# One row of wq loaded in three uneven pieces, and used last

## The chip, the cores and the metric

The kernel runs on one core of one Trainium2 chip. The metric is the device time of one execution in microseconds (us). Three runs of the kernel before took 138.65, 138.70 and 138.75 us; the median is 138.7 us. The profile is one execution taken by the hardware profiler; a time without a unit below is us from the start of its span.

The core has a matrix engine (TensorE, PE), three engines for elementwise work (VectorE or DVE, ScalarE or ACT, GpSimd or POOL) and SyncE (SP), which here only issues transfers. Transfers between the chip's memory and the on-chip buffer of 128 partitions run on 16 DMA engines. A transfer is issued on the queue of SP or ACT and is then split over DMA engines; when an engine has done its share, it adds one count to the transfer's semaphore.

## The reference

One decoding step of a transformer block, batch 4, one new token, model width 1024, 32 query heads in 4 groups of key/value heads, head width 128, all in bfloat16. Cut to what matters:

```python
q = layernorm(x) @ wq                     # wq: 1024 x 4096
k, v = k_cache[:, :, -2048:], v_cache[:, :, -2048:]
p = softmax(q . k / sqrt(128))            # 8 query heads to each kv head
h = x + (p . v) @ wo                      # wo: 4096 x 1024
n = layernorm(h)
out = h + (silu(n @ w1) * (n @ w3)) @ w2  # w1, w3: 1024 x 3584; w2: 3584 x 1024
```

Each weight and each used key and value is read once, 55.6 MB in all, and there are only four rows of activations to multiply them by.

## The kernel before, in words

All large operands go through one tile, `ring`, of five units of 16,384 bfloat16 numbers per partition. A unit is filled again when what it held has been used. In order, SP issues (through the helper `load`, whose only statement is line 124, so that all these transfers carry that line): row 0 of wq (1 MB), rows 1 to 7 of wq (7 MB), four loads of k (2 MB each), two of v, then two more of v, wo (8 MB), w1 and w3 (7 MB each), and w2 in six pieces of 13, 8, 4 and 2 rows and two half rows. "Row" here is an index inside a partition: wq's 1024 input features are dealt so that partition p holds features 8p to 8p+7, and row kc holds feature 8p+kc of every partition; a row of wq is 8,192 bytes in each of the 128 partitions.

The order is written by hand (`manual_schedule`): each engine runs its instructions in program order, and a wait holds all behind it on that engine. SP waits before a load until the unit's old content has been read, and until the semaphore that it will use is free again; there are eight semaphores for transfers, given out in turn to all transfers in the order of the program, x's and the stores' included.

The program's stages:

- x is loaded from ACT's queue into `x_nat` (line 135: four groups of four rows of 512 bytes), transposed (line 218) and normalized in `layernorm_T` (lines 189 to 214), whose result `xn_T` is done by line 211.
- The query (lines 229 to 240): for each of the eight rows kc, two halves of the heads and four column groups, one matmul of 512 columns, 64 in all, accumulating over kc in `q_ps`. In row 0 `start` is set, in row 7 `stop`.
- q is copied (line 243), transposed (line 246) and spread into `Qm` (line 253).
- For each batch element 64 blocks of keys are transposed on PE (line 267) and copied back into the ring (lines 269 and 271), then scores (line 290), softmax (line 331), spreading and transposing of the probabilities (lines 344 and 366) and the output (line 381).
- wo (line 468), the second layernorm, gate and up projections (line 494), and the product with w2 (lines 538 and 554), of which the last rows accumulate in `y_ps`. Then the result is added up (lines 577, 578 and 582) and stored by four small transfers (line 587).

Where the places in the ring meet the change: wq lies in units 0 and 1, rows 0 and 1 in the first half of unit 0. The third and fourth load of v (`load_values(1)`, line 241) overwrite unit 0, the third one rows 0 and 1, the fourth rows 2 and 3. The transfer of w1 begins in unit 1, that of w3 in unit 3, where wo was.

Of the kernel before, what the change touches and what calls it, by code (L numbers as in the profile page):

```python
# [10 lines left out]
P = 128  # L11
# [10 lines left out]
def kernel(  # L22
# [29 lines left out]
    KC = D // P  # L52
# [15 lines left out]
    wq_v = A_wq.rearrange("(p kc) n -> p kc n", kc=KC)  # L68
# [29 lines left out]
    def at(unit, *shape):  # L98
        o = unit * UNIT
        view = ring[:, o : o + int(np.prod(shape))]  # L100
        if len(shape) == 1:
            return view
        names = "abc"[: len(shape)]
        return view.rearrange(
            f"p ({' '.join(names)}) -> p {' '.join(names)}", **dict(zip(names, shape))
        )

    wq_s = at(0, KC, NQ)
# [14 lines left out]
    def load(dst, src):  # L123
        nc.sync.dma_start(out=dst, in_=src)  # L124
# [8 lines left out]
    x_nat = act.tile([P, DQ], BF16)  # L133
    nc.gpsimd.memset(x_nat[:], 0.0)
    nc.scalar.dma_start(out=x_nat[::S, :], in_=x_flat.rearrange("b (c n) -> c b n", c=C))
    for r in (slice(0, 1), slice(1, KC)):
        load(wq_s[:, r, :], wq_v[:, r, :])
    for b in range(B):
        load(k_s[:, b].rearrange("p j d -> p (j d)"), k_v[:, :, b])
    load_values(0)  # L140
# [85 lines left out]

    q_ps = ps.tile([P, 2, REP // 2, Dh], FP32, tag="scA")
    HALF = REP // 2
    for kc in range(KC):
        for hf in range(2):  # L230
            for c in range(C):
                o = (2 * c + hf) * HALF * Dh
                nc.tensor.matmul(  # L233
                    q_ps[R * c : R * c + R, hf],
                    lhsT=xn_T[:, kc, :],
                    rhs=wq_s[:, kc, o : o + HALF * Dh],
                    start=(kc == 0),
                    stop=(kc == KC - 1),
                    tile_position=(0, R * c),
                )  # L240
    load_values(1)
# [198 lines left out]
    for e in range(C):  # L440
# [4 lines left out]
            start=(e == 0),  # L445
            stop=(e == C - 1),
# [6 lines left out]
    for i in range(2):  # L453
        for k in range(2):
# [5 lines left out]
                start=(k == 0),  # L460
                stop=False,
# [3 lines left out]
    for t in range(T):  # L465
        row = wo_s[:, t].rearrange("p (k i n) -> p i k n", k=2, i=2)
        for i in range(2):
# [4 lines left out]
                start=False,  # L472
                stop=(t == T - 1),
# [60 lines left out]
    for w, n in zip(w2_s[:NE], W2B[:NE]):  # L534
        for ff in range(n):
            row = w[:, ff].rearrange("p (k i n) -> p i k n", k=2, i=2)
            for i in range(2):
# [4 lines left out]
                    start=(fc == 0),  # L542
                    stop=(fc == FE - 1),
# [3 lines left out]
    for k in range(2):  # L547
        part = h1[2 * R * k : 2 * R * k + 2 * R, :]
        nc.vector.tensor_tensor(out=part, in0=early_ps[:, k], in1=part, op=ALU.add)
    for m, (w, n) in enumerate(zip(w2_s[NE:], W2B[NE:])):  # L550
        for ff in range(n):
            for t, c, size in ((0, 0, DH), (0, 1, DH), (1, 0, DH), (1, 1, DH), (2, 2, DQ), (2, 3, DQ)):
# [5 lines left out]
                    start=(fc == FE),  # L558
                    stop=(fc == FC - 1),
# [4 lines left out]
        if m == 0:  # L564
# [4 lines left out]
                start=False,  # L569
                stop=False,  # L570
# [3 lines left out]
    for k in range(2):  # L574
        part = slice(2 * R * k, 2 * R * k + 2 * R)
# [44 lines left out]
```

## Time and profile before

| what | us |
|---|---|
| median of three runs | 138.7 |
| the profiled execution's own time | 138.7 |
| its span, first to last instruction | 136.7 |
| PE busy | 74.8 (55%) |
| DVE busy | 49.9 (37%) |
| ACT busy | 28.8 (21%) |
| POOL busy | 15.3 (11%) |
| SP's DMA queue, share of 16 engines' span | 95.3% |
| row 0 of wq, from issue to landing | 4.6 |
| rows 1 to 7 of wq, from issue to landing | 21.2 |
| granted TensorE clock, mean | 0.912 |

The profiled execution is 2.0 us longer than its span; that part lies around the first and the last instruction. A line of the chain reads: start, duration, and what the time went to, an engine's instructions with tile and line or a transfer. A line of the waits names who waited for whom, the total, how often, and the longest. SPq is SP's queue of transfers. Where a line says "q_ps L233 x64", 64 instructions of line 233 of the kernel write the tile `q_ps`.

Besides the views the text uses the trace's records of DMA packets (start, duration, queue and size of each) and the times at which transfers added counts to their semaphores. The records do not name the DMA engine, but a packet starts within some nanoseconds of the end of the one before it on the same engine.

### The profile page before, as it was taken

Reading aid. Unit: us, or ns where it says so; the run is one execution under the profiler, and the core shown is the slowest. Engines: PE = TensorE matmul, PEld = TensorE weight load, DVE = VectorE, ACT = ScalarE, POOL = GpSimd, SP = SyncE. Lnnn points to the kernel's source line nnn. Section 1 sums busy time; section 2 is a strip of 40 time slices with the busy share of each in tenths; the row PEclk is TensorE's granted clock in tenths of the full one; section 3 lists DMA queues with packets and bytes.
Section 4 is the critical chain, followed back from the end, with each engine's and each line's share of the span. In section 5 each row is a group of like instructions: output and inputs, shape, how many; then the busy total and the mean of one; then the engine's idle time right before and its main releaser. Section 6 shows DMA issues by size and latency. Waiting matters only on the chain.

```text
span 136.7 us, 1762 instructions
## 1 busy us (share of the span) xinstructions
PE 74.8 (55%) x762; PEld 40.6 (30%) x762; DVE 49.9 (37%) x50; ACT 28.8 (21%) x32; POOL 15.3 (11%) x41
## 2 busy tenths in 40 slices
PE   0000044959999986029966875994184000946471
PEld 0000011439957852014423323341042000413240
DVE  0000110006526363989799920004100594090022
ACT  3000130025968495104000000000405400000000
POOL 7300060000000000000176333000200000000000
PEclk9999999999999999955999999599959955599999
DMA  4999697999999999998978979969799798999960
GB/s 163 497 454 538 269 537 307 432 417 451 408 432 436 412 436 408 436 585 360 556 326 364 556 326 475 520 285 537 336 470 508 302 520 372 384 423 432 384 245 2
DMA packets 2795, 55.70 MB, mean 408 GB/s; under 512 B 324, under 2 KB 612, under 8 KB 740
## 3 DMA queue, kind: packets, MB, share of 16 engines
q1 hardware_dynamic: 2752, 55.58, 95.3%
q8 instruction: 6, 0.10, 0.3%
q10 hardware_dynamic: 36, 0.01, 0.0%
q14 instruction: 1, 0.01, 0.0%
HBM read 55.58 MB, written 0.01 MB: 407 GB/s over the span
## 4 chain that ended last, share of the span: by engine, by line
DMA 59%; PE 28%; DVE 6%; ACT 3%; SPq 1%; issue 1%; DVEq 0%
DMA ring<-in_B_w_dram 43%; DMA ring<-in_A_wq_dram 15%; PE kt_ps L267 9%; PE sc_ps L290 5%; PE q_ps L233 4%; PE o_ps L381 4%; PE gate L494 3%; DVE P L344 2%; DVE PT L366 2%; ACT ring L271 1%; PE small L381 1%; DVE ring L269 1%; SPq L124 1%; DVE rmax L302 1%; ACT q_sb L243 1%
## 5 line engine op out<-in xcount | busy, mean ns | idle before, releaser
L271 ACT COPY ring<-kt_ps 128x2048 bf16<-128x2048 bf16 x8 | 14.6, 1866 | 7.1 <-PE kt_ps L267 7.1
L267 PE MATMUL kt_ps<-ident,ring 128*128 128x128 bf16 x256 | 15.0, 219 | 0.6 <-DVE Qm L253 0.5
L267 PEld LDWEIGHTS <-ring 128*128 128x128 bf16 x256 | 14.4, 98 | 2.6 <-issue 2.6
L269 DVE COPY ring<-kt_ps 128x2048 bf16<-128x2048 bf16 x8 | 9.8, 1225 | 9.3 <-PE kt_ps L267 9.3
L398 POOL TENSOR_TENSOR o<-od 128x256 f32<-128x256 f32 x4 | 6.8, 1695 | 54.2 <-DVE od L389 54.2
L193 PE MATMUL sums_ps<-both,mean_f 128*128 128x64 f32 x4 | 1.1, 366 | 18.9 <-ACT both L191 18.9
L494 PE MATMUL up<-ring,n_T 128*32 128x448 bf16 x64 | 4.7, 467 | 12.2 <-DMA ring<-in_B_w_dram 12.2
L494 PEld LDWEIGHTS <-n_T 128*32 128x32 bf16 x128 | 4.2, 121 | 20.2 <-DMA ring<-in_B_w_dram 12.7
L344 DVE TENSOR_TENSOR P<-p,gmask 128x2048 bf16<-128x2048 bf16 x4 | 9.1, 2278 | 0.8 <-ACT p L331 0.8
L381 PEld LDWEIGHTS <-PT 128*128 128x128 bf16 x64 | 6.7, 107 | 9.0 <-issue 1.9
L366 DVE STREAM_TRANSPOSE PT<-P 128x2048 bf16<-128x2048 bf16 x4 | 9.2, 2306 | 0.1
L515 DVE RECIPROCAL eg<-eg 128x896 f32<-128x896 f32 x1 | 5.8, 5753 | 9.5 <-ACT eg L514 9.5
L468 PE MATMUL y_ps<-ring,oP 128*32 128x512 bf16 x64 | 8.8, 442 | 0.1
L233 PE MATMUL q_ps<-ring,n_T 128*32 128x512 bf16 x64 | 6.6, 587 | 3.8 <-DMA ring<-in_A_wq_dram 2.0
L381 PE MATMUL o_ps<-ring,PT 128*128 128x512 bf16 x32 | 8.6, 430 | 0.0
L290 PE MATMUL sc_ps<-ring,Qm 128*32 128x512 bf16 x64 | 7.6, 604 | 0.4 <-DVE ring L269 0.4
L538 PE MATMUL early_ps<-ring,hg_T 128*32 128x512 bf16 x42 | 4.9, 379 | 5.1 <-DMA ring<-in_B_w_dram 5.1
L381 PE MATMUL small<-ring,PT 128*128 128x512 bf16 x32 | 7.2, 379 | 0.7 <-DVE rinv L362 0.7
L193 PEld LDWEIGHTS sums_ps<-both,mean_f 128*128 128x128 f32 x4 | 0.8, 248 | 19.4 <-issue 16.9
L494 PE MATMUL gate<-ring,n_T 128*32 128x448 bf16 x64 | 4.6, 458 | 3.2 <-DMA ring<-in_B_w_dram 3.2
L577 ACT CAST res<-y_ps 64x128 bf16<-64x128 f32 x1 | 0.3, 259 | 26.3 <-PE y_ps L554 26.3
L218 DVE STREAM_TRANSPOSE x_T<-x_nat 128x256 bf16<-128x256 bf16 x1 | 0.6, 626 | 13.0 <-DMA x_nat<-in_A_x_dram 13.0
(81 smaller groups left out, 62.5 us busy)
## 6 DMA issues: line engine op xcount, KB each, us to landing
ring<-in_B_w_dram SPq DMA_DIRECT2D x2, 7168.0 KB
ring<-in_A_k_cache_dram SPq DMA_DIRECT2D x4, 2048.0 KB, 25.6
ring<-in_A_v_cache_dram SPq DMA_DIRECT2D x4, 2048.0 KB, 42.9
ring<-in_A_wq_dram SPq DMA_DIRECT2D x1, 7168.0 KB, 21.2
ring<-in_B_w_dram SPq DMA_DIRECT2D x1, 3328.0 KB
ring<-in_B_w_dram SPq DMA_DIRECT2D x1, 2048.0 KB
ring<-in_A_wq_dram SPq DMA_DIRECT2D x1, 1024.0 KB, 4.6
ring<-in_B_w_dram SPq DMA_DIRECT2D x1, 1024.0 KB, 28.1
```

The source lines that it names most:

```text
L233: nc.tensor.matmul(q_ps[R * c : R * c + R, hf], lhsT=xn_T[:, kc, :], rhs=wq_s[:, kc, o : o + HALF * Dh], start=(kc == 0), stop=(kc == KC - 1),
L267: nc.tensor.transpose(out=kt_ps[:, jj], in_=blocks[:, jj, :], identity=ident[:])
L269: nc.vector.tensor_copy(out=blocks, in_=kt_ps[:])
L271: nc.scalar.copy(out=blocks, in_=kt_ps[:])
L290: nc.tensor.matmul(sc_ps[b // 2][R * q : R * q + R, b % 2], lhsT=Qm[:, b, g * R : (g + 1) * R], rhs=kT[:, b, g, q], start=(g == 0), stop=( ...
L344: nc.vector.tensor_tensor(out=P4[:], in0=stage.pop(("p1", b))[:].rearrange("p (x o) -> p x o", o=1).to_broadcast([P, JR * L5, Hkv]), in1=g ...
L366: nc.vector.transpose(out=PT[:].rearrange("p j h -> p (j h)"), in_=stage.pop(("P4", b))[:].rearrange("p x g -> p (x g)"),)
L381: nc.tensor.matmul(o_ps, lhsT=PT[:, i * JM : (i + 1) * JM, :].rearrange("p j h -> p (j h)"), rhs=v_s[b][:, i * JM : (i + 1) * JM, :], star ...
L398: nc.gpsimd.tensor_tensor(out=o2[:], in0=od[:, :2], in1=od[:, 2:], op=ALU.add)
L468: nc.tensor.matmul(y_ps[R * i : R * i + R], lhsT=oP[:, t, :], rhs=row[:, i], start=False, stop=(t == T - 1), tile_position=(0, R * i), ski ...
L494: nc.tensor.matmul(out_ps[hf][R * c : R * c + R, :], lhsT=hn_T[:, kc, :], rhs=cols[:, kc, c, hf], start=(kc == 0), stop=(kc == KC - 1), ti ...
L515: nc.vector.reciprocal(out=eg[:], in_=eg[:])
```

## The change

Row 0 of wq is no longer loaded as one transfer of 128 partitions. Partitions 0 to 95 are loaded first, then rows 1 to 7 in one transfer as before, and then partitions 96 to 120 and 121 to 127 of row 0, each as a transfer of its own, ahead of the keys. The query's matmuls run over rows 1, 2, ... 7 and then 0; `start` and `stop` are set by the position in that order.

```diff
-    for r in (slice(0, 1), slice(1, KC)):
-        load(wq_s[:, r, :], wq_v[:, r, :])
+    PARTS = (slice(0, 96), slice(96, 121), slice(121, P))
+    load(wq_s[PARTS[0], :1, :], wq_v[PARTS[0], :1, :])
+    load(wq_s[:, 1:, :], wq_v[:, 1:, :])
+    for part in PARTS[1:]:
+        load(wq_s[part, :1, :], wq_v[part, :1, :])
     for b in range(B):
         load(k_s[:, b].rearrange("p j d -> p (j d)"), k_v[:, :, b])
     load_values(0)
...
-    for kc in range(KC):
+    for m in range(KC):
+        kc = (m + 1) % KC
         for hf in range(2):
             for c in range(C):
                 o = (2 * c + hf) * HALF * Dh
...
                     rhs=wq_s[:, kc, o : o + HALF * Dh],
-                    start=(kc == 0),
-                    stop=(kc == KC - 1),
+                    start=(m == 0),
+                    stop=(m == KC - 1),
                     tile_position=(0, R * c),
                 )
     load_values(1)
```

SP then has two transfers more, and every transfer behind them uses the semaphore that comes two later in the turn.

## The prediction

> **What bounds the kernel now.** I read four views in this order: the page's slices and DMA queues (is anything full?), the chain that ended last (what sets the end?), SP's waits (is a transfer issued late?), and then the trace's records of single DMA packets and of the counts that each transfer adds to its semaphore when it lands.
>
> The page:
>
> ```profile
> DMA  4999697999999999998978979969799798999960
> DMA packets 2795, 55.70 MB, mean 408 GB/s; under 512 B 324, under 2 KB 612, under 8 KB 740
> q1 hardware_dynamic: 2752, 55.58, 95.3%
> q8 instruction: 6, 0.10, 0.3%
> q10 hardware_dynamic: 36, 0.01, 0.0%
> ```
>
> SP's queue q1 keeps the 16 DMA engines busy for 95.3% of the span, and no compute engine is above 55%. The two small lines matter below: q8 fetched instructions six times, about 16 KB each; q10 is the load of x from ACT's queue.
>
> The chain that ended last:
>
> ```profile
> 1.20 21.18 DMA ring<-in_A_wq_dram
> 22.41 5.59 PE q_ps L233 x55
> 28.03 1.02 ACT q_sb L243
> 30.16 1.96 PE kt_ps L267 x32
> 68.72 30.62 DMA ring<-in_B_w_dram
> 99.48 4.64 PE gate L494 x55
> 104.48 0.43 SPq L124
> 104.96 28.65 DMA ring<-in_B_w_dram
> 133.65 0.30 PE y_ps L554 x2
> 133.97 0.43 DVE res L582
> ```
>
> The reader should see that the end hangs on the last load of w2: from its landing at 133.61 to the span's end at 136.7 are 3.1 us of fixed tail. The pieces with wq and PE in the first 68 us look critical but only decide when w1 is issued. Whether that is in time is told by SP's waits and the landings:
>
> ```profile
> SPq L124 <- DMA ring<-in_A_wq_dram: 16.9, 2, 16.5
> SPq L124 <- PE small L381: 15.2, 1, 15.2
> SPq L124 <- PE y_ps L468: 10.6, 1, 10.6
> SPq L124 <- PE q_ps L233: 2.2, 2, 1.1
> ```
>
> w1 is issued at 68.72 while the load ahead of it (wo) lands from 80.53 on; w3 at 93.0 while w1 lands from 97.48 on. No engine ever runs dry: in the records a packet follows the one before within 4 ns, 309 ns for 8,192 B, 611 ns for 16,384 B, 2,116 to 2,120 ns for 57,344 B. So the time is the length of the longest of 16 queues, plus start and tail.
>
> And the queues are not equally long. Row 0 of wq adds its 16 counts between 4.90 and 5.30. The last load of w2 adds nine counts at 131.75 to 131.96, then one at 132.18, one at 132.94, and five at 133.47 to 133.61. The steps arise at the instruction fetches: after those at 34.07, 40.74, 50.54, 82.50 and 105.63 one more engine each is some 1.7 us behind for good, and a fetch of 8 KB at 119.12 costs another 0.9. Five engines of 16 hold the kernel back by 1.65 us (133.61 less 131.96).
>
> **The change, part by part.**
>
> *Row 0 in loads of 96, 25 and 7 partitions.* No byte more or less; only which engine carries it. A load over 128 partitions adds 16 counts. The x load, outermost extent 4, adds four as its data lands (15.68 to 15.73, one more coming early, at 2.27), and so do the stores of 4 rows. So a transfer uses as many engines as divide its rows: 16 for 96 (6 rows each), 5 for 25 (5 each), 7 for 7 (1 each). I take it that every transfer on fewer engines begins at the same first engine, so that x's four are among the five; were it otherwise, the sum below has the same terms on other queues. Bounds for the 25: one engine alone (25 rows by 0.309, 7.7 us) to all 16 (0.6 us); the row of four on four is nearest, hence five. [...]
>
> Rows of 8 KB per engine, before and after: engines 0 to 4 go from 8 to 6+5+1 = 12, which is 4 by 0.309 = +1.24 us; engines 5 and 6 from 8 to 7, -0.31; engines 7 to 15 from 8 to 6, -0.62. As no queue runs dry, this shift stays to the end.
>
> *What that does to the last landing* depends on which engines are the late ones. The records don't name engines, but the four that carry x can be followed by their packets: x is queued on them between 6.75 and 15.41. The fetches at 34.07 and 50.54 hit engines without x. For the other three and the one at 119.12 the queues have crossed within a nanosecond too often to say.
> - A fetch engine among the first five: 133.61 + 1.24 = 134.85, that is +1.24.
> - Only the one of 132.94 among them: 134.18, +0.57.
> - None: the first five end at 131.96 + 1.24 = 133.20, the late ones at 133.61 - 0.62 = 132.99 (133.30 if one is engine 5 or 6): -0.3 to -0.4.
>
> Counted blindly, of the 13 engines not excluded, three late ones by fetches avoid nearly five places with a chance of about 0.2 (8.25/13 by 7.25/12 by 6.25/11). Five fetches on five different engines look like a walk in order, and two of the walk lie outside the first four, which raises it. I put about 0.4 on none.
>
> *Two more DMAs on SP.* One issue takes 0.41 us (wq) to 0.65 (k) on SP, and 1.11 on ACT for x on four engines: +0.8 to +2.2, so k's issue moves from 1.66 to at most 3.9. wq's rest feeds the queues until 21.7; cost 0. The eight semaphores are dealt in turn, so the fourth k load now waits for the 96 partitions (about 4.7), the first v load for x (15.73), the second for wq's rest (about 22 instead of 5.3). Behind these on SP stand only later loads; what is queued lasts until 41 and more, so 0. The third v load overwrites row 0, whose matmuls now come last: from 23.5 to about 28.2, due at 51. Cost 0.
>
> *q's matmuls, row 0 last.* Before, its 8 matmuls ran at 19.34, ahead of the wait for the rest. Now all 64 follow the rest, which lands 0.62 earlier (six rows ahead of it, not eight): 22.37 - 0.62 + 5.59 + 8 by 0.1 = 28.14 instead of 28.00. The two small loads end on the first engines near 21.5 + 6 by 0.309 = 23.3, needed at 27.3. x on those engines alternates with packets of 2.12 us; even one round lost puts the normalized x at 20.8, before 21.75.
>
> *Attention.* The second k load ends up to 1.1 later than 32.17 and is wanted at about 32.2; so PE may run 1.1 late. w1 has 10 us of slack (69.9 against 80), w3 about 2.3 (94.2 against 97.1 less 0.6 of start). Cost 0; gone if PE slips by over 2.3.
>
> **The sum.** The profiled run took 138.7 (span 136.7 plus 2.0 around it), which is the median too. I forecast the first case: 138.7 + 1.24 = 139.9; its own range is 139.7 to 140.1.
>
> **The rivals.**
> - *The queues are evened out* (the other side). For it: 1.86 us (1.24 + 0.62) are moved between groups whose ends lie 1.65 apart, and both fetches that can be placed miss the first four. Against it: three cannot be placed, and engine 4 carries no x. Its place is the last w2 landing, it decides if all five fetches hit engines 5 to 15. 133.2 to 133.3 instead of 133.61: 138.3 to 138.4, say 138.35.
> - *Only the fetch at 119.12 hits one of the five*: 139.3.
> - *A row written by an engine other than its usual one is dearer.* [...] For it: 2 packets of wq beside x's stray 512 B rows took 2,136 and 2,156 ns. Against it: beside x's third round none took over 2,124. Six rows by 0.309 on top: 131.96 + 1.24 + 1.85 = 135.05, that is 140.1; with 96 rows taking as long as 128 (+0.62), 140.8. Say 140.4. [...]
> - *The engines are dealt otherwise*, or the gain and loss cancel: 138.5 to 138.9. Nothing speaks for an even deal but that x has only four rows to a group.
>
> **How the numbers follow.** No change is told from 138.7 to within about 0.2% (0.28 us). Chances: forecast 0.36; 119.12 alone 0.08; dearer rows 0.15; evened out 0.34; dealt otherwise 0.07. Slower: 0.36 + 0.08 + 0.15 = 0.59. The evened case lies at the bound, so 0.30 of its 0.34 is faster and 0.04 same; with 0.07, same is 0.11 and faster 0.30. The range takes in the evened case below and the dearer rows above: 138.2 to 140.8, with less than 2 in 10 outside.
>
> **What will show it.** In the changed trace: the 25-partition load adds five counts, the 7-partition load seven, the rest of wq lands near 21.75, q's matmuls end near 28.1. At the last w2 load five counts should stand 1.24 later relative to the others; if one lies at 134.8 the forecast is right, if all lie below 133.4 the evened case. Packets of k near 22 us over 620 ns would mean dearer rows. I am wrong altogether if the queues run dry (idle DMA before 97), or if the fetches move.

## The result, and the profile after

The changed kernel takes 142.64 us (median, 142.48 to 142.78), the kernel before 138.68 beside it: the ratio is 1.0286, with a 95% interval of 1.0268 to 1.0303. It is 3.96 us slower. The direction was forecast, the size was not: 139.9 was predicted and 140.8 was the upper end of the range. The profiled execution took 142.48, with a span of 140.4.

The page of the changed kernel, slices and DMA queues:

```profile
DMA  5999698999999999999999969979979979999940
GB/s 145 357 507 524 261 523 208 320 434 429 397 443 429 411 429 425 439 401 551 448 448 392 504 296 495 490 327 490 490 310 495 474 310 429 427 421 401 409 175 2
DMA packets 2807, 55.70 MB, mean 397 GB/s; under 512 B 336, under 2 KB 624, under 8 KB 752
q1 hardware_dynamic: 2764, 55.58, 95.0%
```

The reader should see two things. The engines are as busy as before (95.0% of the span against 95.3%) with the same 55.58 MB, so nothing ran dry: the same bytes simply took longer. And in the seventh and eighth slice (21 to 28 us) the rate falls to 208 and 320 GB/s. This is where the two small loads and the first load of k run. The same place by stage, and ahead of it the stage in which row 0 lands, first for the kernel before, then for the changed one; the last two columns are the DMA engines' busy share (a packet counts where it starts, so it can pass 1) and the rate in GB/s:

```profile
2.00:5.00 3.00, 0.00 (x0) 0.00 (x0) 0.19 (x1) 1.28 (x1) 2.18 (x13) 1.00 1.54 636
22.00:24.00 2.00, 1.59 (x16) 0.68 (x19) 0.00 (x0) 0.00 (x0) 0.00 (x0) 1.00 0.96 410
24.00:26.00 2.00, 2.00 (x24) 0.90 (x20) 0.00 (x0) 0.00 (x0) 0.00 (x0) 1.00 0.98 418
```

```profile
2.00:5.00 3.00, 0.00 (x0) 0.00 (x0) 0.19 (x1) 1.28 (x1) 2.16 (x13) 1.00 1.53 497
22.00:24.00 2.00, 0.52 (x8) 0.27 (x11) 0.00 (x0) 0.00 (x0) 0.00 (x0) 1.00 1.08 266
24.00:26.00 2.00, 2.00 (x25) 0.76 (x21) 0.00 (x0) 0.00 (x0) 0.00 (x0) 1.00 1.15 254
```

The engines are just as busy and move 266 and 254 GB/s instead of 410 and 418; in the first stage the 96 rows run at 497 GB/s where 128 ran at 636. In the records, the packets of 16,384 B (k's) that start between 22.5 and 25.5 us take 1,113 to 1,331 ns, but for one of 1,480, where they took mostly 611 and at most 695 before. Of the 32 small rows of 8,192 B the first seven take 311 to 362 ns, the 25 behind them 539 to 632, where a row took 309. Both on the five engines with the small rows and on the eleven others everything runs at about half speed.

The chain of the changed kernel, cut to seven of its pieces:

```profile
3.03 33.36 DMA ring<-in_A_k_cache_dram
36.43 3.75 PE kt_ps L271 x64
71.55 30.52 DMA ring<-in_B_w_dram
102.20 4.90 PE gate L498 x54
107.94 29.26 DMA ring<-in_B_w_dram
137.25 0.30 PE y_ps L558 x2
137.57 0.43 DVE res L586
```

A load of k has taken the place of wq and the query at the head of the chain. The end has the same form as before: last w2 landing (137.20), then PE, DVE and the stores. The last landing moved by 3.59 us, from 133.61. The covers that the prediction named held: w1 is issued at 71.55 while wo lands from 83.05 on, w3 at 94.16 while w1 lands from 100.00 on. PE waits for k, which it did not before:

```profile
PE kt_ps L271 <- DMA ring<-in_A_k_cache_dram: 2.1, 2, 1.2
PE q_ps L237 <- DMA ring<-in_A_wq_dram: 5.3, 1, 5.3
```

That is lost time on PE, but w1 and w3 were still issued in time, so it costs nothing.

The counts of the transfers, from the records (before, then changed):

```
row 0, 128 rows  4.90 to 5.30           96 rows  5.41 to 5.83
rest of wq      21.91 to 22.37                   22.42 to 22.87, one at 23.43
25 rows                                 five counts, 25.59 to 26.08
7 rows                                  two at 23.18 and 23.70, five at 26.33 to 26.84
first k         26.85 to 27.27          eleven at 29.34 to 29.82, five at 31.21 to 31.42
last w2         nine 131.75 to 131.96   six at 134.28 to 134.60
                132.18, 132.94          nine at 135.78 to 136.33
                five 133.47 to 133.61   one at 137.20
```

### The profile page after: what moved, and what is told of

Same layout as the page of the kernel before. It is cut to its first block, busy times and chain, and to the rows that moved or that the text cites. A ratio compares the mean times of both kernels' runs of the same rounds, so it can differ in the third digit from the quotient of the medians.

```text
span 140.4 us, 1765 instructions
## 1 busy us (share of the span) xinstructions
PE 72.8 (52%) x762; PEld 40.4 (29%) x762; DVE 50.1 (36%) x50; ACT 28.8 (20%) x32; POOL 15.3 (11%) x41
## 3 DMA queue, kind: packets, MB, share of 16 engines
q1 hardware_dynamic: 2764, 55.58, 95.0%
HBM read 55.58 MB, written 0.01 MB: 396 GB/s over the span
## 4 chain that ended last, share of the span: by engine, by line
DMA 66%; PE 22%; DVE 6%; SPq 2%; issue 1%; ACT 1%
DMA ring<-in_B_w_dram 43%; DMA ring<-in_A_k_cache_dram 24%; PE kt_ps L271 7%; PE sc_ps L294 5%; PE o_ps L385 4%; PE gate L498 3%; SPq L124 2%; DVE P L348 2%; DVE PT L370 2%; PE small L385 1%; DVE ring L273 1%; DVE rmax L306 1%; ACT p L335 1%; PE small L308 1%; DVE qmax L310 0%
## 5 line engine op out<-in xcount | busy, mean ns | idle before, releaser
L237 PE MATMUL q_ps<-ring,n_T 128*32 128x512 bf16 x64 | 5.4, 510 | 5.3 <-DMA ring<-in_A_wq_dram 5.3
L472 PE MATMUL y_ps<-ring,oP 128*32 128x512 bf16 x64 | 7.1, 379 | 0.1
```

The costliest lines, as they stand in the source:

```text
L237: nc.tensor.matmul(q_ps[R * c : R * c + R, hf], lhsT=xn_T[:, kc, :], rhs=wq_s[:, kc, o : o + HALF * Dh], start=(m == 0), stop=(m == KC - 1 ...
L472: nc.tensor.matmul(y_ps[R * i : R * i + R], lhsT=oP[:, t, :], rhs=row[:, i], start=False, stop=(t == T - 1), tile_position=(0, R * i), ski ...
```

## The experiments

Three theories stand against each other. A: only the length of the queues counts, a row costs 0.309 us wherever it goes. B: a row is dear when an engine writes it into partitions that another engine normally fills, and slows that engine too. C: any load that runs on few engines is dear in itself. Which engine normally fills which partitions is theory B's own assumption, and so are the "groups", "places" and "owners" of the expectations: the records name neither engine nor partition, and no run shows them. The medians of the kernel before, run beside each of these, were 138.65 to 138.75.

### The order of the matmuls alone

```diff
+    for r in (slice(0, 1), slice(1, KC)):
+        load(wq_s[:, r, :], wq_v[:, r, :])
...
+    for m in range(KC):
+        kc = (m + 1) % KC
```

> Row 0 is loaded first and whole, as before; only the order of the query's matmuls is the changed one. All theories: 138.7 to 138.9. The matmuls end 0.5 to 0.8 us later than before (all 64 behind the landing of the rest, near 28.7), which the slack ahead of w1 and w3 hides. Over 139.2 would mean that the order itself has a part in the 3.9 us.

Measured: 138.77, ratio 1.0017 (0.9991 to 1.0042). The query's matmuls end at 28.24, where they ended at 28.00, and the order costs nothing that can be told. So the 3.96 us have to come from the loads.

### Uneven pieces, even queues

```diff
-    PARTS = (slice(0, 96), slice(96, 121), slice(121, P))
+    PARTS = (slice(0, 96), slice(96, P))
```

> Row 0 by loads of 96 and 32 partitions, the 32 behind the rest of wq: every engine carries 8 rows again (6 and 2), so no queue is longer than before. Theory A (only the queue lengths count, each row at 0.309 us): 138.7. Theory B (rows written by engines other than the partition's usual one run at half speed, and slow the usual ones): the 96 land near 5.4 to 5.8 as in the changed kernel, the 32 slow the start of k, 139.7 to 140.5. Theory C (a load on few engines slows all): the 32 use 16 engines, so only the 0.5 us of the 96 stay, about 139.2.

Measured: 140.76, ratio 1.0146 (1.0131 to 1.0161). The stage from 22 to 24 us, in which the 32 rows run, with the same columns as above:

```profile
22.00:24.00 2.00, 0.55 (x8) 0.30 (x11) 0.00 (x0) 0.00 (x0) 0.00 (x0) 1.00 1.00 262
```

Again busy engines at 262 GB/s. Theory A is out: no queue is longer than before, and half of the loss is there. The 96 land at 5.45 to 6.10, later than 128 rows do; the first k at 28.81 to 29.16 instead of 26.85 to 27.27. Theory B has the direction but was priced too low, by 0.3 us.

### The small pieces in low partitions

```diff
+    PARTS = (slice(32, P), slice(0, 25), slice(25, 32))
```

> The pieces lie elsewhere: 96 are partitions 32 to 127, 25 are 0 to 24, 7 are 25 to 31. Each engine carries as many rows as in the changed kernel. Theory B: the first five engines now write mostly partitions that are theirs in the 128-partition loads, so beside them k's packets on the other engines stay near 611 ns instead of 1,150 to 1,250, and the small rows take near 0.31 to 0.4 us; 140 to 141. Theory C (which partitions does not matter): as the changed kernel, 142.4 to 142.9, k's packets near 1,200 ns.

Measured: 141.76, ratio 1.0213 (1.0195 to 1.0231): between the two. The records tell where the difference lies. While the 25 rows run into partitions 0 to 24, small rows take mostly 0.35 to 0.45 us and k's packets mostly 690 to 830 ns. Later, with the 7 rows going into partitions 25 to 31, the fifteen packets of k that start between 24.1 and 24.9 take 1,218 to 1,469 ns. So it counts which partitions are written, and the seven rows on seven neighbours slow k's packets more than the 25 do.

### The small pieces ahead of the rest of wq

```diff
+    for part in PARTS:
+        load(wq_s[part, :1, :], wq_v[part, :1, :])
+    load(wq_s[:, 1:, :], wq_v[:, 1:, :])
```

> The changed kernel with the two small loads directly behind the 96, ahead of the rest of wq. Queue lengths are those of the changed kernel. Theories B and C: the same slowdown, now beside wq's 57,344-byte packets, which take more than 2,120 ns on all or most engines; 142.4 to 142.9. If the slowdown belongs to k's loads (their rows come from other places in memory), the rest's packets stay at 2,120 and the time falls to 140 to 141.

Measured: 142.85 from two runs (142.24 and 143.45), ratio 1.0298 (1.0243 to 1.0352), like the changed kernel. Now wq's packets suffer: eleven take 3,724 to 4,605 ns instead of 2,120, and k's stay at 612 to 621. It is not a property of k's loads.

### One load's worth of rows, three ways

These three, and all runs below but the one with row 0 in halves, add a load to the kernel before, behind the rest of wq, into a part of the ring that the first two loads of v fill later; nobody reads it. This prices a load by itself.

```diff
+    spare = at(2, NQ)
+    load(spare[0:16, :], wq_v[0:16, 0, :].rearrange("(c b) n -> c b n", c=4))
```

> The kernel before with one more load behind the rest of wq: row 0 of partitions 0 to 15 once more, into partitions 0 to 15 of a part of the ring that is not yet in use, in four groups of four, so on four engines with four rows each. Nobody reads it. [...] Four engines get 1.24 us more: 138.7 if they are all early ones, up to 139.3 if the one of 132.94 is among them. Theory C (any load on few engines slows all): k's packets near 1,200 ns, 140 to 141.

> The same with the same bytes read, but written into partitions 64 to 79. Theory B: the four engines write to partitions of four others: rows at about 0.6 us, k's packets on at least those four owners, or on all engines, at 1,100 to 1,250 ns; 139.9 to 141.5. If what counts is where the bytes are read, it is as the load into 0 to 15.

> The same with the rows of partitions 64 to 79 read and written into 0 to 15. Theory B: as the load of 0 to 15 into 0 to 15, 138.7 to 139.3, k's packets at 611 to 625 ns. If the place in memory counts, it is as slow as the load into 64 to 79.

Measured: 140.00, 140.17 and 140.03, ratios 1.0094, 1.0106 and 1.0096 with intervals of about 0.003 to either side. The runs did not do what was planned: the load added sixteen counts, so it ran on sixteen engines with one row each, and not on four. All three cost the same, 1.35 to 1.5 us, for 0.31 us of queue. So it mattered neither whether rows 0 to 15 or 64 to 79 were read nor which of these two groups of neighbours was written. The rows' own packets took mostly 309 ns; k's packets right behind took mostly 1,330 to 1,610 (twelve of sixteen 1,428 to 1,534 in the first of the three runs), and k landed some 1.3 us late. The stage of the first of the three:

```profile
22.00:24.00 2.00, 0.74 (x8) 0.31 (x11) 0.00 (x0) 0.00 (x0) 0.00 (x0) 1.00 0.89 246
```

Two microseconds at 246 GB/s instead of 410 make the delay. It is about what four rows one behind the other take (4 by 0.309 = 1.24 us), though each engine had only one; why was not shown. Whether it hangs on the rows being neighbours was tested with runs below.

### Row 0 in halves

```diff
+    for part in (slice(0, 64), slice(64, P)):
+        load(wq_s[part, :1, :], wq_v[part, :1, :])
```

> Row 0 by two loads of 64 partitions, both ahead of the rest; 4 and 4 rows per engine, 8 as before; the matmuls in the changed order. Theory B: half of the engines write to partitions not theirs all the time, two at each place: packets of 8,192 bytes near 620 ns, so 128 rows take about 5 us instead of 2.5 and everything behind is about 2.5 us late: 141.0 to 141.5. Theory A (queue lengths only): 138.7 to 138.9.

Measured: 141.31, ratio 1.0188 (1.0159 to 1.0218), as theory B has it. The second half lands at 7.61 to 8.16 where 128 rows land at 4.90 to 5.30, and the median packet of 8,192 B takes 616 ns. The view by stage of this run:

```profile
2.00:5.00 3.00, 0.00 (x0) 0.00 (x0) 0.19 (x1) 1.28 (x1) 2.15 (x13) 1.00 1.01 238
```

The engines are busy throughout, and the loads over 64 partitions move 238 GB/s, where the load over 128 moved 636.

### The same rows spread, and the same bytes in narrow strips

```diff
+    load(spare[0:P:8, :], wq_v[0:P:8, 0, :])        # first run
+    load(spare[:, :512], wq_v[:, 0, :512])          # second run
```

> The extra 16 rows once more, one on each engine, now into every eighth partition (0, 8, ... 120). [...] So k's first load lands 0.6 to 0.8 later than before instead of 1.3, the time is 139.3 to 139.5. Theory D (any extra load of 16 rows costs a fixed 1.3 us): 140.0.

> The same 128 KB extra, as 1,024 bytes in each of the 128 partitions. Theory B: every engine writes only to its own group, 8 KB more each: 0.31 to 0.4 us, 139.0 to 139.1. Theory D: 140.0.

Measured: 139.36 (ratio 1.0042, 1.0023 to 1.0062) and 139.21 (1.0037, 1.0021 to 1.0052). The first run has 16 rows on sixteen engines, as the three above. Spreading them over every eighth partition halves the price: k lands 0.6 to 0.8 us late instead of 1.3, and its first packets take 790 to 920 ns instead of some 1,450. That is the delay that was forecast; why spreading halves it was not shown. In 128 strips nothing is held up at all, k's packets stay at 611 to 627; k lands 0.3 to 0.5 us late, and eight strips of 46 ns to an engine are 0.37. The same stage of the two runs, which stand at 369 and at 485 GB/s, where sixteen neighbours stood at 246:

```profile
22.00:24.00 2.00, 1.31 (x16) 0.57 (x19) 0.00 (x0) 0.00 (x0) 0.00 (x0) 1.00 0.98 369
```

```profile
22.00:24.00 2.00, 1.41 (x16) 0.67 (x19) 0.00 (x0) 0.00 (x0) 0.00 (x0) 1.00 1.15 485
```

### The changed kernel's 25 rows alone, and spread

```diff
+    load(spare[96:121, :], wq_v[96:121, 0, :])      # first run
+    load(spare[0:121:5, :], wq_v[0:121:5, 0, :])    # second run
```

> The kernel before with one extra load, the changed kernel's 25 partitions (96 to 120) of row 0, into a part of the ring not yet in use: what that load costs alone. It should add five counts. Theory B: five rows at about 0.62 us on five engines, k's packets on the others near 1,200 ns meanwhile; the five are 3.1 us later, and with the engine of 132.94 among them the time is 140.8 to 141.4. Bare queue length would be 1.55 us more on five engines, 139.5.

> [...] Theory B: at most 0.5 us lost on engines that only own a group, small rows at 0.31 to 0.45 us, 139.5 to 140.2. If only the number of engines matters, it is as the 25 neighbours.

Measured: 141.28 (ratio 1.0181, 1.0151 to 1.0211) and 140.65 (1.0136, 1.0106 to 1.0165). The first is as expected: five counts, small rows near 0.63 us, k's packets 1,100 to 1,240, and the five engines land k at 29.99 to 30.12, 3 us late. The second missed: most of the spread rows still take 0.49 to 0.55 us and k's packets mostly 970 to 1,050. Rows in every fifth partition thus lost 1.9 us (140.65 against 138.75), where as many neighbours lost 2.5. Being neighbours is not the whole price; what the rest is was not shown. The stage of the first run, 1.18 busy at 262 GB/s:

```profile
22.00:24.00 2.00, 1.56 (x16) 0.69 (x19) 0.00 (x0) 0.00 (x0) 0.00 (x0) 1.00 1.18 262
24.00:26.00 2.00, 2.00 (x24) 0.92 (x20) 0.00 (x0) 0.00 (x0) 0.00 (x0) 1.00 0.80 303
```

### Are few engines dear in themselves, and who is held up?

The first run adds four loads of five rows each (partitions 0, 4, ... 16, then 1, 5, ... 17, and so on), the second one load of seven rows (0, 4, ... 24), the third one of the seven neighbours 121 to 127.

```diff
+    for j in range(4):                                          # first run
+        load(spare[j : j + 17 : 4, :], wq_v[j : j + 17 : 4, 0, :])
...
+    load(spare[0:25:4, :], wq_v[0:25:4, 0, :])                  # second run
...
+    load(spare[121:P, :], wq_v[121:P, 0, :])                    # third run
```

> [...] Theory B: rows at 0.31 us, k's packets on the other eleven engines at 611 to 625 ns, the five engines 1.24 later and the others not at all; with the engine of 132.94 among the five the last landing is 134.2 and the time 139.3. Theory C (few engines make a load dear): k's packets near 1,000 to 1,200 ns, 140.5 to 141.5.

> [...] Theory B: k's packets stay at 611 to 625 ns everywhere, seven engines 0.31 later, 138.7 to 139.0 (138.8 if the engine of 132.94 or a fetching one is among them).

> [...] If only the owners of the two places and the seven writers are held up, seven engines keep 611 to 625 ns; if a full place holds up everybody, all sixteen are slow and the time is 139.6 to 140.1.

Measured: 139.59 (ratio 1.0061, 1.0038 to 1.0084), 138.93 (1.0015, 1.0003 to 1.0026) and 139.75 (1.0069, 1.0046 to 1.0091). The stages of the first and of the third run:

```profile
22.00:24.00 2.00, 1.59 (x16) 0.67 (x19) 0.00 (x0) 0.00 (x0) 0.00 (x0) 1.00 0.99 422
```

```profile
22.00:24.00 2.00, 0.74 (x8) 0.33 (x11) 0.00 (x0) 0.00 (x0) 0.00 (x0) 1.00 0.78 254
```

Twenty rows on five engines, in loads whose rows step by four, leave the rate at 422 GB/s: all 20 rows take 309 ns, and k's packets that start up to 24 us take 611 to 641. In the second run the seven rows take 309 ns too, and k's packets from 21.5 to 26 us at most 739, where the kernel before has one of 725. Seven neighbouring rows bring the rate down to 254. There the seven rows' own packets take 309 ns, but of the sixteen packets of k that follow or run beside them one takes 872 ns and fifteen take 1,180 to 1,582. Sixteen is every engine, and nine of them had no small row at all.

So theory C is out. Theory B's times came out in these three runs, but for 0.3 us in the first; what it assumes of engines and partitions stays unshown. It needs an addition: seven neighbouring rows hold up nine engines that carry none of them. What these share with the seven is not shown by any run; that stays open.

One rival remains to be weighed. In these runs the rows read step like the partitions written, so that neighbours might be slow to read and not slow to write; no run changes the step of one without the other. The counts speak for writing. In both runs with seven rows the rows' packets end on time, at 21.95 to 22.20 with steps of four and at 21.92 to 22.15 with neighbours. But the counts, which tell that the data has landed, come at 22.36 to 22.54 in the one and at 23.28 to 23.75 in the other. What is late with neighbours comes behind the packet's own 309 ns.

The first run also bears out the bookkeeping of queues, though its time is 0.3 us above the 139.3 expected; the last landing, at 134.25, is only 0.1 above. Four rows of 0.309 us on five engines are 1.24 us. k lands 1.2 us late on five engines and on time on eleven, and the last w2 counts are six at 131.72 to 132.17, nine at 133.02 to 133.51, and one at 134.25. That last one is the engine of 132.94 plus 1.24 (134.18): it is among the first five. The five late ones of 133.47 to 133.61 have not moved by 1.24 (five of the nine stand at 133.33 to 133.51): none of them is.

## Why the prediction was wrong

**What failed** is the term "4 by 0.309 = +1.24 us" for engines 0 to 4 and, with it, "-0.62" for engines 7 to 15. A row was priced at its time on its engine's queue. That price held for the 20 rows in loads that step by four (309 ns each). For the rows of this change the runs showed this in its place:

- The load of 96 rows was to be 0.62 shorter than that of 128. It landed 0.5 us later instead (5.41 to 5.83 against 4.90 to 5.30), which is 1.13 us off, on all engines. Its packets took a median of 486 ns, against 309. The reason was not shown.
- The six small rows were to take 6 by 0.309 = 1.86. By their packets they took 3.2 to 3.3 us on each of the five engines (from 22.03 to 22.15 up to 25.23 to 25.46). By the counts, from the rest's landing near 22.6 to the five last ones near 26.6, it was about 4.0. k, which was to come 1.24 late on these engines, came 4.2 late (31.21 to 31.42 against 26.85 to 27.27).
- The other engines were to gain 0.62 and lost 2.5 (first k at 29.34 to 29.82 instead of 26.85 to 27.27): 0.5 from the 96 rows, 2.0 while the small rows ran.

The engine that now ends last had its last count at 132.94 before, and 132.94 + 4.26 = 137.20 is the new end. That makes 3.59 us on the last landing. The tail behind it grew from 3.06 to 3.24 us, for a reason not looked into, and the profiled run is 0.16 below the median; together that is the 3.96 of the medians.

The prices of the runs add up to it as well: 0.5 us for the 96 rows, 2.5 for the 25 alone and 1.0 for the 7 alone are 4.0. They need not add up so closely, since the two small loads run beside each other.

**The forecast case's premise was wrong.** It took one of the five fetching engines to be among the first five. In the changed kernel that would show as a count near 133.5 + 4.2 = 137.7. There is none; the nine counts at 135.78 to 136.33 are four of the first five and the five that fetched. That its direction came out was luck: slower came from another cause. Instead, the engine of the fetch at 119.12 is among them, the case that had 0.08.

**The evened-out rival's condition was met,** and it still did not come. All five fetches hit engines outside the first five, and the queues were moved against each other nearly as planned: nine of the engines now end within 0.55 us of each other. But moving 1.86 us between the queues cost 2.5 us or more on every engine. By the prediction's own sums it would not have come either: with the engine of 132.94 among the first five, 139.3 was due.

**The dearer rows are what happened.** The rival had 0.15 and 140.4. Its sign came too: packets of k near 22 us over 620 ns were to mean dearer rows, and they take 1,113 and more. It doubled the six rows (+1.85, where packets and counts show +1.4 to +2.1) and let 96 rows last as long as 128 (+0.62), on an engine that ended at 131.96: 135.67. No run shows either term as such: of the small rows seven took 311 to 362 ns and 25 took 539 to 632, and the 96 rows took 3.58 us where 128 took 3.19. Two things lacked: the 96 rows last 0.5 longer than 128, and the last of the five starts 0.98 later. 135.67 + 0.5 + 0.98 = 137.15.

The rival's weak chance rests in part on a misread row. It was held against it that none of wq's packets beside x's third round, at 11.03 to 11.09, took over 2,124 ns. But the packets that start at 11.12 and 11.31 took 2,142 and 2,131. After the fourth round, at 13.16 to 13.23, three packets that start between 13.18 and 13.44 took 2,225 to 2,274. Only after the second round, at 8.9, did none take over 2,122. The trace before thus spoke more for the rival than the prediction says.

**What was right.** No queue runs dry, so a shift at 25 us is still there at 137. The 25 rows ran on five engines and the 7 on seven, as their counts show. The order of the matmuls costs nothing (1.0017 with the order alone). The waits that moved to other semaphores and the later issues on SP left no queue empty (95.0% busy); no run times them alone. The rest of wq was forecast near 21.75 and came at 22.42 to 23.43.

## What to carry to other kernels

While transfers over all 128 partitions keep the engines busy (95% here), a piece of a load over a few neighbouring partitions uses no idle time: here its rows took up to 632 ns instead of 309, and k's packets, on the engines without such rows too, 1,113 to 1,480 ns between 22.5 and 25.5 us instead of mostly 611. Price such a load by a run and not by rows per engine: 25 rows are 1.55 us on each of five engines by the row (5 by 0.309), and cost 2.5 as neighbours and 1.9 in every fifth partition. Cut loads by columns over all 128 partitions; the 128 strips cost little more than their bytes (0.46 us against 0.37), where the same bytes in sixteen neighbouring rows cost 1.35 to 1.5. When the rows must be few, let the row numbers step by four from 0: in the run with seven such rows k's packets took at most 739 ns and in the kernel before at most 725, and in the run with twenty they took 611 to 641 up to 24 us.

## What the runs showed that was not expected

- Seven neighbouring rows slow every engine: seven rows of 8 KB (56 KB) into partitions 121 to 127 took nine engines without any of them from 611 ns to between 872 and 1,582 for the packet at hand, and cost 1.0 us in all.
- 96 partitions are slower than 128 in absolute terms: 96 rows from first packet to last end took 3.58 us (1.754 to 5.338), 128 rows 3.19 us (1.768 to 4.956).
- A source cut into four groups of four neighbouring rows did not make a load run on four engines; it added sixteen counts. x's load, whose four groups are not runs of neighbouring rows in memory, added four.
